# A second expert whose output product becomes seven block products in a phase of its own per token group

## The chip, the cores and the metric

The kernel runs on one core of one Trainium2 chip, as one launch. The metric is the device time of that launch in microseconds (us); the runs shown are medians. TensorE is called PE, VectorE DVE, ScalarE ACT, GpSimd POOL, and SyncE, which issues the DMAs, SP.

## What is computed

Attention without a softmax, then two experts one after the other on 2304 tokens of 512 values. All inputs and outputs are float32:

```python
ret = scores * Dmat                       # batch 4, 8 heads, 576 tokens, 64 values a head
x = transpose(ret @ v)                    # 2304 tokens x 512
h = x @ w_in                              # first expert, 2048 hidden
x = (h * cos(h)) @ w_out
xn = x / sqrt(mean(x * x) + 1e-6) * rms_g # second expert, 1536 hidden
silu = g * sigmoid(g)  where  g = xn @ w_gate
out = (silu * (xn @ w_val)) @ w_out
```

## The kernel before

**Precision.** Each float32 factor is split into a rounded high part (a cast on ACT) and the rest (a subtraction on DVE, the helper `minus`, line 124). A product is three matmuls: high by high, high by low, low by high.

**Stages.** Attention comes first. The first expert then takes the tokens in five tiles (four of 512, one of 256); in its second and third tile it also turns the second expert's weights from 64-bit words into float32 values, which it stores in DRAM (`piece_steps`). In the last tile of the first expert (five steps of ACT and DVE work beside each hidden block, `other_steps`, from a list `ready`) the second expert's first operands and weights are made.

**Second expert, gate and value.** Three groups of 768 tokens, each in two halves of 384. A group has twelve *quads* `q`, even ones for the gate, odd ones for the value. A quad gives two blocks of 128 hidden features by two token halves, from 512 inputs, and does this 2x2 block product with seven block products (line 745) in place of eight: six matmuls of 384 columns each. They go to two PSUM banks, alpha and beta. Between them alpha is copied out by ACT (s1, s2, s4; line 752), DVE adds a sum to a bank (lines 765 and 772), ACT applies Silu (767) and DVE multiplies by it (773). Where a product starts a bank anew, or adds to it after a copy, it waits for the reader. A quad's weights are three plain blocks and four sums, each as high and low part (768 KB and 1024 KB). In group 0 they are made while the quads run, two ahead (`quad_steps`: casts lines 509 and 524, subtractions, four small sums on DVE), and stored; groups 1 and 2 load them again (543), one quad ahead, into two sides.

**Second expert, output.** After each gate and value pair `j`, the four products are split into high and low parts (777, 124), and the pair's output product is 36 matmuls of 512 columns (`out_n`, line 717), into six banks that stay open through the group. They are emitted in pieces between the products of the *next* two quads (`fills`): nine, nine, nine, and the rest.

**Order.** In the second expert PE, ACT, DVE and POOL are given their instructions in the order of the code; only between the two parts of the program may rows move. SP's DMAs are placed by a scheduler. An engine runs its row strictly in order, so a waiting instruction holds those behind it.

## Time and profile before

| | |
|---|---|
| Median of 3 runs | 926.82 us (925.85 to 929.55) |
| Profiled execution, span | 923.1 us (first to last instruction; 3.7 us below the median of the runs) |
| PE busy | 900.4 us, 98% of the span, 4996 matmuls |
| DVE, ACT, POOL busy | 615.7, 462.1, 29.3 us |
| Second expert | 493.49 us to the end |
| Granted clock of TensorE | 0.999 of its full 2.4 GHz |

A row of the timeline gives start, length, engine, line, operation and count; `[0.57 <-ACT s L752]` is idle time before it and what ended it. Matmuls overlap: a matmul's length is longer than the distance to the next start, and the distance is the pace.

### The profile page before, as it was taken

Reading aid. Unit: us, or ns where it says so; the run is one execution under the profiler, and the core shown is the slowest. Engines: PE = TensorE matmul, PEld = TensorE weight load, DVE = VectorE, ACT = ScalarE, POOL = GpSimd, SP = SyncE. Lnnn points to the kernel's source line nnn. Section 1 sums busy time; section 2 is a strip of 40 time slices with the busy share of each in tenths; the row PEclk is TensorE's granted clock in tenths of the full one; section 3 lists DMA queues with packets and bytes.
Section 4 is the critical chain, followed back from the end, with each engine's and each line's share of the span. In section 5 each row is a group of like instructions: output and inputs, shape, how many; then the busy total and the mean of one; then the engine's idle time right before and its main releaser. Section 6 shows DMA issues by size and latency. Waiting matters only on the chain.

```text
span 923.1 us, 12892 instructions
## 1 busy us (share of the span) xinstructions
PE 900.4 (98%) x4996; PEld 789.8 (86%) x4996; DVE 615.7 (67%) x1022; ACT 462.1 (50%) x816; POOL 29.3 (3%) x27
## 2 busy tenths in 40 slices
PE   7899999999999999999999999999999999999998
PEld 6788888888887888988887899999888999999997
DVE  3999989678888887668667666675456445333332
ACT  4666576576556665467544444444342334322222
POOL 2321100000000000000000000000000000000000
PEclk9999999999999999999999999999999999999999
DMA  9966261136525443202045376666744555755531
GB/s 333 411 222 252 98 251 47 34 126 195 170 68 173 146 157 115 62 2 102 1 173 181 141 300 252 252 264 248 253 181 177 207 204 215 264 206 206 206 129 68
DMA packets 34732, 163.72 MB, mean 177 GB/s; under 512 B 4080, under 2 KB 5232, under 8 KB 23792
## 3 DMA queue, kind: packets, MB, share of 16 engines
q1 hardware_dynamic: 34672, 162.91, 48.5%
q8 instruction: 39, 0.64, 0.3%
q14 instruction: 21, 0.17, 0.1%
HBM read 123.57 MB, written 39.32 MB: 176 GB/s over the span
## 4 chain that ended last, share of the span: by engine, by line
PE 66%; DVE 24%; ACT 6%; issue 3%; DMA 1%; SPq 0%; ACTq 0%; DVEq 0%
PE h L745 27%; PE acc L717 16%; PE acc L187 6%; PE acc L188 6%; PE acc L189 6%; DVE t L142 3%; DVE r L422 3%; DVE r L416 2%; DVE glo L124 2%; DVE t L143 2%; ACT ghi L424 2%; PE h L189 2%; PE h L187 2%; PE h L188 2%; DVE t L137 2%
## 5 line engine op out<-in xcount | busy, mean ns | idle before, releaser
L745 PE MATMUL h<-w 128*128 128x384 f32 x1224 | 230.5, 337 | 6.6 <-ACT s L752 2.6
L745 PEld LDWEIGHTS h<-w 128*128 128x128 f32 x1224 | 215.0, 188 | 15.2 <-ACT s L752 5.3
L717 PE MATMUL acc<-w,shi 128*128 128x512 f32 x432 | 134.4, 392 | 0.0
L187 PE MATMUL acc<-ghi,w 128*128 128x512 f32 (+1 forms) x320 | 117.4, 373 | 2.9 <-ACT xall L615 1.9
L188 PE MATMUL acc<-glo,w 128*128 128x512 f32 (+1 forms) x320 | 117.8, 369 | 0.1
L189 PE MATMUL acc<-ghi,w 128*128 128x512 f32 (+1 forms) x320 | 117.4, 368 | 0.0
L752 ACT COPY s<-h 128x384 f32<-128x384 f32 x108 | 51.8, 479 | 128.0 <-PE h L745 127.9
L717 PEld LDWEIGHTS acc<-w,shi 128*128 128x128 f32 x432 | 80.1, 188 | 13.5
L418 ACT ACTIVATE r<-r,half_pi 128x512 f32<-128x512 f32 (+1 forms) x80 | 54.5, 681 | 68.7 <-DVE r L416 68.2
L765 DVE TENSOR_TENSOR sg<-s,h 128x384 f32<-128x384 f32 x54 | 29.9, 553 | 85.4 <-PE h L745 45.7
L717 PE MATMUL acc<-w,slo 128*128 128x512 f32 x216 | 85.4, 395 | 0.0
L777 ACT CAST shi<-v 128x384 fp32r<-128x384 f32 x72 | 37.1, 515 | 70.0 <-DVE v L773 70.0
L187 PEld LDWEIGHTS acc<-ghi,w 128*128 128x128 f32 x320 | 59.4, 188 | 14.7 <-ACT xall L615 2.9
L124 DVE TENSOR_TENSOR glo<-r,ghi 128x512 fp32r<-128x512 f32 (+1 forms) x78 | 49.6, 636 | 33.5 <-ACT ghi L424 31.7
L424 ACT CAST ghi<-r 128x512 fp32r<-128x512 f32 (+1 forms) x80 | 46.2, 578 | 50.7 <-DVE r L422 49.5
L188 PEld LDWEIGHTS acc<-glo,w 128*128 128x128 f32 x320 | 60.3, 188 | 10.2 <-DVE glo L124 0.3
L189 PEld LDWEIGHTS acc<-ghi,w 128*128 128x128 f32 x320 | 60.3, 189 | 10.1
L124 DVE TENSOR_TENSOR slo<-v,shi 128x384 fp32r<-128x384 f32 x72 | 40.1, 557 | 37.3 <-ACT shi L777 37.3
L772 DVE TENSOR_TENSOR v<-s,h 128x384 f32<-128x384 f32 x54 | 29.8, 552 | 52.0 <-PE h L745 37.9
L745 PE MATMUL h<-b,w 128*128 128x384 f32 x288 | 56.7, 338 | 0.0
L188 PE MATMUL h<-xlo,w 128*128 128x512 f32 (+1 forms) x148 | 54.3, 367 | 0.1
L189 PE MATMUL h<-xhi,w 128*128 128x512 f32 (+1 forms) x148 | 54.2, 366 | 0.0
(105 smaller groups left out, 1514.2 us busy)
## 6 DMA issues: line engine op xcount, KB each, us to landing
w<-s SPq DMA_DIRECT2D x24, 1024.0 KB, 4.8
raw<-w_dram SPq DMA_DIRECT2D x36, 512.0 KB, 4.0
w<-w SPq DMA_DIRECT2D x18, 1024.0 KB, 5.0
w<-s SPq DMA_DIRECT2D x24, 768.0 KB, 6.4
raw<-w_dram SPq DMA_DIRECT2D x16, 1024.0 KB, 7.3
x<-qkv_dram SPq DMA_DIRECT2D x15, 1024.0 KB, 11.5
s<-w SPq DMA_DIRECT2D x12, 1024.0 KB, 4.8
s<-w SPq DMA_DIRECT2D x12, 768.0 KB, 3.7
```

The lines of the kernel that those rows point to most:

```text
L124: eng.tensor_tensor(dst, src, hi.bitcast(F32), op=ALU.subtract)
L187: nc.tensor.matmul(dst, a[0], b[0], start=start, stop=False)
L188: nc.tensor.matmul(dst, a[0], b[1], start=False, stop=False)
L189: nc.tensor.matmul(dst, a[1], b[0], start=False, stop=stop)
L418: nc.scalar.activation(r, r, AF.Sin, bias=half_pi, scale=1.0)
L424: nc.scalar.copy(hi, r)
L717: nc.tensor.matmul(acc, (hi, hi, lo)[k][:, c], w[:, u, (0, 1, 0)[k], :], start=start and u == 0 and k == 0, stop=stop and u == 1 and k == 2)
L745: nc.tensor.matmul(bank, a[:, wp], xp[:, c], start=start and kc == 0 and n == 0, stop=kc == 1 and n == 2, skip_group_check=True)
L752: nc.scalar.copy(t, alpha)
L765: nc.vector.tensor_tensor(t, s, bank, op=ALU.add)
L772: nc.vector.tensor_tensor(t, s, bank, op=ALU.add)
L777: nc.scalar.copy(hi, t)
```

## The change

The output product now also is a 2x2x2 block product done with seven block products, once per token group after its twelve quads (`whole_out`). The three halved dimensions are the tokens (two halves of 384), the hidden features (the two blocks of each pair) and the outputs (two halves of 256). One block product (`out_product`) is six feature blocks by three token blocks by three parts: 54 matmuls of 256 columns. The group's 24 gated blocks are kept in a float32 tile `SV`; `out_split` makes the high and low parts of two of its blocks (768 columns), and `out_difference` makes four differences over the tile (128x2304 each), three on DVE and one on POOL. `block_out` adds the sums and sends the output; `s1`, `s2`, `s4` are as in a quad.

The output weights are made once, as three plain blocks and four sums of each pair, in the last tile of the first expert (`out_steps`, six of them, ahead of the steps for quads 0, 1 and 2) and stored in DRAM as seven parts of 1536 KB. The small sums move from DVE to POOL. There are now three sides; `fetch(n + 3)` loads quads and output parts alike, three items ahead. Quads have no fills: `quad` stops twice (`yield`), and the loop runs quad `q`'s products 3 to 5, then products 1 and 2 of quad `q+1`, then products 6 and 7 of `q`; neighbours use two different pairs of banks. The normalisation steps for later groups go in at the hooks.

```diff
         yield
-        if before is not None:
-            minus(nc.vector, w[:, 1].bitcast(F32R), hi, z)
-            nc.sync.dma_start(store[before // 2][:, before % 2], w.bitcast(F32))
         yield
...
+    def operand_weights(q, plain, sums, keep):
+
+        def high0():
+            z = values_of[q]
+            nc.scalar.copy(plain[:, 0], z[:, :3])
+
+        def low0():
+            z = values_of[q]
+            minus(nc.vector, plain[:, 1], plain[:, 0], z[:, :3])
+            for dst, a, b, op in ((4, 0, 3, ALU.subtract), (3, 3, 2, ALU.add), (0, 3, 0, ALU.subtract), (1, 1, 0, ALU.subtract)):
+                nc.gpsimd.tensor_tensor(z[:, dst], z[:, a], z[:, b], op=op)
+
+        def high1():
+            z = values_of[q]
+            for n in range(2):
+                nc.scalar.copy(sums[:, 0, 2 * n:2 * n + 2], z[:, 3 * n:3 * n + 2])
+
+        def low1():
+            z = values_of.pop(q)
+            for n in range(2):
+                minus(nc.vector, sums[:, 1, 2 * n:2 * n + 2], sums[:, 0, 2 * n:2 * n + 2], z[:, 3 * n:3 * n + 2])
+            keep()
+
+        return [("A", high0), ("D", low0), ("A", high1), ("D", low1)]
...
+    def out_steps(j):
+
+        plain = late["pw"].tile([P, 2, 3, 2 * P], F32R, tag="pw", name="pw")
+        sums = slots[0].rearrange("p a b c -> p (a b c)").rearrange("p (h n c) -> p h n c", h=2, n=4)
+
+        def keep():
+            for n, part in enumerate([plain[:, :, n] for n in range(3)] + [sums[:, :, n] for n in range(4)]):
+                nc.sync.dma_start(kept_out[OUT_PLACES[n]][:, :, j], part.bitcast(F32))
+            fetch_next()
+
+        return operand_weights(3 * j + 2, plain, sums, keep)
...
-    def ahead(n):
...
+    def ahead(i, n):
...
+        if 0 < n <= 2 * NPR:
+            j, half = divmod(n - 1, 2)
+            if not half:
+                late["out"] = out_steps(j)
+            ready.extend(late["out"][2 * half:2 * half + 2])
+        if 1 <= n < 8:
             ready.append(late["steps"].pop(0))
             while late["steps"] and late["steps"][0][0] != "A":
                 ready.append(late["steps"].pop(0))
...
+        if n in (11, 13, 14):
+            late["quad"] = quad_steps((11, 13, 14).index(n))
+            ready.extend(late["quad"][:2])
+        if n in (12, 13, 14):
+            ready.extend(late["quad"][2:])
...
+    while ready:
+        ready.pop(0)[1]()
...
+        alpha, beta = (t[:, :HALF] for t in banks())
...
+            dst = SV[:, j, u, h]
...
+                    nc.vector.tensor_tensor(dst, s, bank, op=ALU.add)
+                nc.scalar.activation(dst, bank if s is None else dst, AF.Silu)
+            else:
+                if s is not None:
+                    t = gp.tile([P, HALF], F32, tag="v", name="v")
                     nc.vector.tensor_tensor(t, s, bank, op=ALU.add)
...
+                    bank = t
+                nc.vector.tensor_tensor(dst, bank, dst, op=ALU.mult)
...
         product(alpha, plain[:, :, 0], 0, True)
-        s1 = keep("s1")
-        also("s1")
+        s1 = sums_of("s1", alpha)
         product(beta, plain[:, :, 1], 1, True)
-        r11 = result(0, 0, s1, beta)
-        next(r11)
-        also("m11")
+        result(0, 0, s1, beta)
+        hook("r11")
+        yield
         product(alpha, sums[:, :, 0], 2, False)
-        s2 = keep("s2")
-        next(r11)
-        also("r11")
+        s2 = sums_of("s2", alpha)
+        hook("s2")
         product(beta, sums[:, :, 3], 3, True)
         product(alpha, sums[:, :, 2], 4, False)
-        s4 = keep("s4")
-        also("s4")
-        r22 = result(1, 1, s4, beta)
-        next(r22)
-        also("m22")
-        next(r22)
-        also("r22")
-        fills(9)
+        s4 = sums_of("s4", alpha)
+        result(1, 1, s4, beta)
+        hook("r22")
+        yield
         product(alpha, sums[:, :, 1], 5, False)
-        r12 = result(0, 1, None, alpha)
-        next(r12)
-        next(r12)
+        result(0, 1, None, alpha)
         product(beta, plain[:, :, 2], 6, False)
-        r21 = result(1, 0, s2, beta)
-        next(r21)
-        also("m21")
-        next(r21)
-        fills(9 if q % 2 == 0 else 36)
-        also("end")
-
-    fill = []
...
+    def out_split(k, i):
+        a, b = BLOCK_OF[k]
+        src = SV[:, 2 * i:2 * i + 2, a, b, :]
+        t = places.pop(0)
+        split_out.setdefault(k, []).append(t)
+        nc.scalar.copy(t[:, 0], src)
+        minus(nc.vector, t[:, 1], t[:, 0], src)
+
+    def out_difference(eng, dst, a, b):
+        x = lambda ab: SV[:, :, ab[0], ab[1], :]
+        eng.tensor_tensor(x(dst), x(a), x(b), op=ALU.subtract)
+
+    def out_product(g, k, pair, start):
+
+        n = g * ITEMS + NQUAD + OUT_ORDER.index(k)
+        w = side_out(n)
+        home = split_out.pop(k)
+
+        def product(i, m):
+            s, wi = home[i // 2], w[i // 3][:, :, i % 3]
+            bank = pair[m // 2][:, m % 2 * 2 * P:(m % 2 + 1) * 2 * P]
+            for p, (a, b) in enumerate(((0, 0), (0, 1), (1, 0))):
+                nc.tensor.matmul(bank, s[:, a, i % 2, m * P:(m + 1) * P], wi[:, b],
+                                 start=start and i == 0 and p == 0 and m % 2 == 0, stop=i == NPR - 1 and p == 2,
+                                 skip_group_check=True)
+
+        last = g == NGROUP - 1 and k == OUT_ORDER[-1]
+        for i, m in [(i, m) for m in range(3) for i in range(NPR)] if last else [(i, m) for i in range(NPR) for m in range(3)]:
+            product(i, m)
+        places.extend(home)
+        fetch(n + 3)
...
+    def whole_out(g):
+
+        s = operand_steps(g + 1) if g + 1 < NGROUP else []
+        alpha, beta = [acc_tile(0), acc_tile(1)], [acc_tile(2), acc_tile(3)]
+        out_product(g, 0, alpha, True)
+        out_split(1, 2)
+        for i in range(3):
+            out_split(5, i)
+        s1 = sums_out("s1", alpha)
+        out_difference(nc.vector, (0, 0), (0, 1), (0, 0))
+        out_difference(nc.vector, (0, 1), (1, 1), (0, 1))
+        out_difference(nc.vector, (1, 1), (1, 1), (0, 0))
+        out_difference(nc.gpsimd, (1, 0), (1, 0), (1, 1))
+        out_product(g, 1, beta, True)
+        for i in range(3):
+            out_split(2, i)
+        block_out(g, 0, 0, s1, beta)
+        gamma = banks()
+        out_product(g, 5, gamma, True)
+        for i in range(3):
+            out_split(3, i)
+        out_product(g, 2, alpha, False)
+        for i in range(3):
+            out_split(4, i)
+        s2 = sums_out("s2", alpha)
+        out_product(g, 3, beta, True)
+        for i in range(3):
+            out_split(6, i)
+        plus(s2, s2, beta)
+        run(s[:9])
+        out_product(g, 4, alpha, False)
+        s4 = sums_out("s4", alpha)
+        block_out(g, 0, 1, s4, gamma)
+        block_out(g, 1, 1, s4, beta)
+        run(s[9:16])
+        delta = banks()
+        out_product(g, 6, delta, True)
+        block_out(g, 1, 0, s2, delta)
+        run(s[16:])
+
+    for g in range(NGROUP):
+
+        pending = []
+
+        def hook(q, at):
...
+            if g == 0 and 0 < q < NQUAD - 2 and at in ("s2", "r21"):
+                if at == "s2":
+                    pending[:] = quad_steps(q + 2)
+                run(pending[:2])
+                del pending[:2]
+            if q in (5, 10) and at == "r22":
+                out_split(0, q // 7)
+            if q == NQUAD - 1:
+                if at == "r11":
+                    out_split(0, 2)
+                elif at == "r22":
+                    out_split(1, 0)
+                    out_split(1, 1)
+            elif g < 2:
+                idle(1, "P") if at == "s2" else None
+                idle(2, "AD")
...
+        now = quad_of(0)
+        next(now)
+        for q in range(NQUAD):
+            next(now)
+            then = quad_of(q + 1) if q + 1 < NQUAD else None
+            if then:
+                next(then)
+            next(now)
+            now = then
...
+        if g + 1 < NGROUP:
+            assert len(normal) == (3, 5)[g], (g, normal, len(background))
+        whole_out(g)
```

**PE, the second expert's first quads and an output phase.** Before: quads 0 and 1 and most of 2 in one run on banks `h`, then the output product in pieces.

```order
L189 MATMUL acc<-ghi,w 128x512
L745 MATMUL h<-w 128x384 x114
L717 MATMUL acc<-w,shi 128x512 x2
L717 MATMUL acc<-w,slo 128x512
L717 MATMUL acc<-w,shi 128x512 x2
L717 MATMUL acc<-w,slo 128x512
L717 MATMUL acc<-w,shi 128x512 x2
L717 MATMUL acc<-w,slo 128x512
L745 MATMUL h<-w 128x384 x12
L717 MATMUL acc<-w,shi 128x512 x2
L717 MATMUL acc<-w,slo 128x512
L717 MATMUL acc<-w,shi 128x512 x2
```

Now: quads alternate between the bank pairs `h` and `acc`; the last 30 are products 3 to 7 of quad 11, and behind them stand the 378 matmuls of the output phase of 256 columns.

```order
L194 MATMUL acc<-ghi,w 128x512
L763 MATMUL h<-w 128x384 x30
L763 MATMUL acc<-w 128x384 x12
L763 MATMUL h<-w 128x384 x12
L763 MATMUL acc<-w 128x384 x18
L763 MATMUL h<-w 128x384 x12
L763 MATMUL acc<-w 128x384 x12
```

```order
L763 MATMUL h<-w 128x384 x18
L763 MATMUL acc<-w 128x384 x12
L763 MATMUL h<-w 128x384 x12
L763 MATMUL acc<-w 128x384 x30
L828 MATMUL acc<-w 128x256 x18
L828 MATMUL acc<-w,b 128x256 x18
L828 MATMUL acc<-w 128x256 x72
L828 MATMUL h<-w 128x256 x54
L828 MATMUL acc<-w 128x256 x18
```

The pieces between the quads are gone, and the matmuls of 256 columns stand behind the whole group.

**ACT, the start of the second expert.** Before (`z` holds weight values; `w` are quad 2's weights, made last; quads 0 and 1 were made earlier):

```order
L424 CAST ghi_4417<-r_4416 128x512
L653 ACT_TABLE_LOAD
L653 ACTIVATE spare_83<-half_pi_81 128x1
L509 CAST w_4446<-z_4339 128x768
L524 CAST w_4460<-z_4339 128x512 x2
L752 COPY s1_4524<-h_4516 128x384
L752 COPY s2_4540<-h_4516 128x384
L767 ACTIVATE sg_4532<-sg_4532 128x384
L752 COPY s4_4555<-h_4516 128x384
L615 COPY xall_84<-acc_3935 128x512
L767 ACTIVATE sg_4558<-sg_4558 128x384
```

Now (`w_4308`, `w_4359` quad 0; `w_3937<-z_4435` the last output block; `w_4404`, `w_4459` quad 1; `w_4550` quad 2):

```order
L682 ACT_TABLE_LOAD
L682 ACTIVATE spare_83<-half_pi_81 128x1
L514 CAST w_4308<-z_4491 128x768
L525 CAST w_3937<-z_4435 128x512 x2
L525 CAST w_4359<-z_4491 128x512 x2
L748 COPY s1_4637<-h_4629 128x384
L773 ACTIVATE SV_4628<-SV_4628 128x384
L748 COPY s2_4653<-h_4629 128x384
L748 COPY s4_4667<-h_4629 128x384
L773 ACTIVATE SV_4628<-SV_4628 128x384
L644 COPY xall_84<-acc_3921 128x512
L514 CAST w_4404<-z_4534 128x768
```

The casts of quad 0 now stand directly ahead of its first copy, and those of quad 1 behind quad 0's fourth bank copy, a Silu and a copy to `xall`.

**ACT, a gate quad followed by a value quad.** Before, in group 1 (`s1` to `s4` of both quads, Silu on `sg`, casts of the products `shi`):

```order
L752 COPY s1_5922<-h_5914 128x384
L752 COPY s2_5938<-h_5914 128x384
L767 ACTIVATE sg_5930<-sg_5930 128x384
L752 COPY s4_5953<-h_5914 128x384
L767 ACTIVATE sg_5955<-sg_5955 128x384
L767 ACTIVATE sg_5973<-h_5914 128x384
L767 ACTIVATE sg_5981<-sg_5981 128x384
L752 COPY s1_6014<-h_6006 128x384
L752 COPY s2_6031<-h_6006 128x384
L777 CAST shi_6033<-v_6022 128x384
L752 COPY s4_6049<-h_6006 128x384
L777 CAST shi_6059<-v_6051 128x384
```

Now, at the end of group 0, quads 10 (`h_5320`) and 11 (`acc_5393`); the casts from `SV` to `b_5366` and `w_3990` are `out_split(0, 1)` and `(0, 2)`:

```order
L525 CAST w_3937<-z_5217 128x512 x2
L748 COPY s2_5373<-h_5320 128x384
L748 COPY s4_5387<-h_5320 128x384
L773 ACTIVATE SV_4628<-SV_4628 128x384
L811 CAST b_5366<-SV_4628 128x768
L748 COPY s1_5401<-acc_5393 128x384
L811 CAST w_3990<-SV_4628 128x768
L773 ACTIVATE SV_4628<-h_5320 128x384
L773 ACTIVATE SV_4628<-SV_4628 128x384
L748 COPY s2_5437<-acc_5393 128x384
L748 COPY s4_5451<-acc_5393 128x384
```

The copies s1 and s2 of the value quad now stand behind a cast of 768 columns each, and s2 behind the gate quad's last two Silus as well.

## Rows read from the trace of the kernel before

**Rows 1.** Page, part 1: busy us, share of the span, instructions.
```profile
PE 900.4 (98%) x4996; PEld 789.8 (86%) x4996; DVE 615.7 (67%) x1022; ACT 462.1 (50%) x816; POOL 29.3 (3%) x27
```

**Rows 2.** Lines by form, PE: shapes, count, busy us, mean ns, idle before.
```profile
L745 PE MATMUL h<-w 128*128 128x384 f32 x1224 | 230.5, 337 | 6.6 <-ACT s L752 2.6 <-DVE sg L765 2.5 <-DVE v L772 0.9
L717 PE MATMUL acc<-w,shi 128*128 128x512 f32 x432 | 134.4, 392 | 0.0
...
L717 PE MATMUL acc<-w,slo 128*128 128x512 f32 x216 | 85.4, 395 | 0.0
L745 PE MATMUL h<-b,w 128*128 128x384 f32 x288 | 56.7, 338 | 0.0
```

**Rows 3.** Timeline, PE, second expert in full swing: start us, length.
```profile
523.73 0.63 PE L717 MATMUL acc<-w,shi 128*128 128x512 f32 x2
...
525.81 5.41 PE L745 MATMUL h<-w 128*128 128x384 f32 x30
531.06 0.63 PE L717 MATMUL acc<-w,shi 128*128 128x512 f32 x2
```

**Rows 4.** Timeline, PE, first expert's tile of 256 tokens.
```profile
363.89 0.28 PE L187 MATMUL h<-xhi,w 128*128 128x256 f32 x1
...
366.77 0.28 PE L187 MATMUL acc<-xhi,w 128*128 128x256 f32 x1
```

**Rows 5.** Timeline, PE, start and end of the second expert.
```profile
493.49 5.70 PE L745 MATMUL h<-w 128*128 128x384 f32 x30
499.76 3.40 PE L745 MATMUL h<-w 128*128 128x384 f32 x18 [0.57 <-ACT s L752]
...
519.54 0.63 PE L717 MATMUL acc<-w,shi 128*128 128x512 f32 x2
...
919.20 0.39 PE L717 MATMUL acc<-w,slo 128*128 128x512 f32 x1
```

**Rows 6.** Lines by form, ACT.
```profile
L752 ACT COPY s<-h 128x384 f32<-128x384 f32 x108 | 51.8, 479 | 128.0 <-PE h L745 127.9
...
L767 ACT ACTIVATE sg<-sg 128x384 f32<-128x384 f32 x54 | 28.4, 526 | 28.8 <-DVE sg L765 28.5
...
L562 ACT CAST w<-xall 128x768 fp32r<-128x768 f32 x17 | 14.1, 829 | 0.0
L524 ACT CAST w<-z 128x512 fp32r<-128x512 f32 x24 | 13.7, 618 | 14.1 <-DVE z L518 14.1
```

**Rows 7.** Lines by form, DVE.
```profile
L773 DVE TENSOR_TENSOR v<-v,sg 128x384 f32<-128x384 f32 x54 | 30.1, 558 | 1.9
...
L124 DVE TENSOR_TENSOR w<-xall,w 128x768 fp32r<-128x768 f32 x17 | 16.3, 956 | 1.7 <-ACT w L562 1.5
```

**Rows 8.** Timeline, PE and ACT, near the end.
```profile
899.72 2.27 PE L745 MATMUL h<-w 128*128 128x384 f32 x12
901.04 0.48 ACT L752 COPY s<-h 128x384 f32<-128x384 f32 x1 [2.09 <-PE h L745]
```

**Rows 9.** Timeline, POOL and DVE, attention stage.
```profile
36.27 1.08 POOL L244 TENSOR_TENSOR x<-x,gk_sb 128x512 f32<-128x512 f32 x1 [4.24 <-DMA x<-qkv_dram]
...
36.49 1.95 DVE L142 SCALAR_TENSOR_TENSOR t<-raw,t 128x1024 int32<-128x1024 int32 x1
...
46.86 1.23 DVE L142 SCALAR_TENSOR_TENSOR t<-raw,t 128x1024 int32<-128x1024 int32 x1
```

**Rows 10.** DMA issues: count, KB each, median us from issue to landing.
```profile
w<-s SPq DMA_DIRECT2D x24, 1024.0 KB, 4.8
...
w<-s SPq DMA_DIRECT2D x24, 768.0 KB, 6.4
...
z<-w SPq DMA_DIRECT2D x12, 512.0 KB, 5.7
```

**Rows 11.** Windows: engines' busy us, granted clock, DMA share, GB/s.
```profile
480.00:493.00 13.00, 13.00 (x59) 10.78 (x58) 10.28 (x18) 8.04 (x12) 0.00 (x0) 1.00 0.66 250
520.00:535.00 15.00, 15.00 (x79) 13.90 (x78) 11.89 (x23) 6.24 (x13) 0.00 (x0) 1.00 0.86 333
```

More of the change, by code (lines that the diff above doesn't have):

```diff
@@ L536, in quad_steps @@
[L536 to L548 removed]
+        def keep():
+            for part, dst in zip((plain, sums), kept[q]):
+                nc.sync.dma_start(dst, part.bitcast(F32))
+            fetch_next()
```

324 lines of the change are left out of this document (131 added, 193 removed).

## The prediction

> **What bounds the kernel now.** I read the page's shares first: PE is busy 900.4 of 923.1 us, against 615.7 for DVE, 462.1 for ACT and 29.3 for POOL [rows 1]. So the time is PE's work plus the holes in it. The timeline of PE gives the paces that the work is made of [rows 3]: nine matmuls of 512 columns between 523.73 and 525.81, 0.231 us each, and thirty of 384 between 525.81 and 531.06, 0.175 us each. Changes of shape inside a stretch cost nothing that shows.
>
> The second expert starts at 493.49; its last matmul ends at 919.20 + 0.39 = 919.59 [rows 5], so it lasts 426.1 us. It holds 1224 + 288 = 1512 matmuls of 384 columns and 432 + 216 = 648 of 512 [rows 2]: 1512 x 0.175 + 648 x 0.231 = 264.6 + 149.7 = 414.3 us. Waits are the remaining 11.8 us. The lines by form name what ended them: ACT's copies, DVE's sums [rows 2]. 114 matmuls stand before 519.54: 26.05 us for 19.95 of work [rows 5], so 6.1 of the 11.8 lie in the first three quads, and 5.7 in all the rest.
>
> **PE's work after.** The 1512 stay. The 648 go, and 3 groups x 7 products x 54 = 1134 of 256 columns come. The only rows with that width are in the first expert: 24 in 366.77 - 363.89 = 2.88, or 0.120 us each [rows 4]. Then 1134 x 0.120 = 136.1, against 149.7: **13.6 us less**. The break-even is 149.7 / 1134 = 0.132 us. Bounds for the pace: half of 512's, 0.1155 (another 5 us gained), and 384's, 0.175 (62 lost); I take 0.120, from the same width.
>
> A rule speaks against this step. The Trainium skill, "TensorE: Matmul & The Clock Gate", section "Back-to-back issue gap", gives 81 ns sustained for 128 columns and 131 ns for 512; a straight line between them gives an estimate of 98 ns for 256. By it the new work is 1134 x 0.098 = 111 us and the old 648 x 0.131 = 85, so the change would add 26 us in place of taking 13.6. The trace does not agree with these figures: 512 columns take 231 ns here and 256 take 120.
>
> **What the fills covered.** A product of six is 6 x 0.175 = 1.05 us. A bank's result is visible 0.27 us after its product's nominal end: the six of the row at 899.72 end at 900.77, the copy starts at 901.04 [rows 8]. Copies take 0.48, Silu 0.53, a cast of 768 columns 0.83, of 512 columns 0.62, a subtraction of 768 columns 0.96, an add of 384 about 0.56 [rows 6, 7]. A copy therefore frees its bank 0.27 + 0.48 after the product. The next product in that bank stands one product later (1.05) in the run 3, 4, 5: nothing lost if ACT is free. Now 36 matmuls of 512 columns no longer stand between; two products of the neighbour quad do, 2.1 us.
>
> *A. The first quads.* PE reaches quad 0 with no weights lying ready; before, two quads had them. Taken along ACT's new row: quad 0's first cast waits for its values, whose load takes 5.7 us [rows 10] and is issued behind the output blocks' stores: 1.5 lost (0 to 4). The second cast, behind POOL's small sums: 1.0. Quad 1's cast stands behind quad 0's s4 copy, a Silu and the copy to `xall`: 0.27 + 0.48 + 0.56 + 0.53 + about 0.6, then 0.83 for the cast and 0.96 for the low part [rows 6, 7], 4.2 in all, of which 3.9 on PE. Quad 3's cast waits for its load in front of quad 1's copies: 1.8. With 0.3 of small ones 8.5 (bounds 5 to 12) in place of 6.1: **+2.4**.
>
> *B. Group 0's value quads 3, 5, 7 and 9.* ACT has a Silu and two weight casts ahead of s2: 0.27 + 0.56 + 0.53, then 2 x 0.62, then the copy, 3.0 to 3.1 after the third product, where the fifth wants it after 2.1 (the neighbour's two lie between). 0.9 x 4 = **+3.6** (0, if the Silu's input is early, to 6).
>
> *C. Each group's end.* Quad 11 has no neighbour behind it. ACT's row between its first products is the cast of `out_split(0, 2)` (0.83), then its low part on DVE (0.96), the add (0.56), the Silu (0.53), s2 (0.48): the copy is done about 4.0 after the third product where 2.1 is there, 1.9 lost; the sixth product then waits 0.27 + 0.48 for s4, 0.75. In `whole_out` ACT's casts have 6.48 us a product (54 x 0.120), far more than they need. DVE has three differences of 2304 columns: 0.558 for 384 [rows 7], and from 384 to 768 columns 0.398 more (956 - 558), so 0.558 + 5 x 0.398 = 2.54 each. The POOL difference is 4.5 times the 512-wide row of 1.08 [rows 9], 4.9. I get the low part of block 2 ready 27.9 us after quad 11's third product starts, where PE wants it at 27.6: 0.3. That is 1.9 + 0.75 + 0.3 = 2.9, three times: **+8.7** (0, if quad 11's queue is hidden, to 15).
>
> *D. The rest.* The old 5.7 us go with the order they came from; the normalisation steps at the hooks are still there, so I keep 2.0: **-3.7** (-5.7 to 0).
>
> **Costed at nothing.** The output weights' casts, subtractions and seven stores per pair in the first expert's last tile: PE fills 13.00 of 13.00 us there, with DVE at 10.28 and ACT at 8.04 [rows 11], so each has 2.7 to 5 us in 13 free. If that cover is short, 0 to 3 lost. The last output is read from its bank and stored as before.
>
> **Weights.** Groups 1 and 2 load every quad as before, 768 + 1024 KB (1.835 MB), but a quad now lasts 7 x 1.05 = 7.35 us: 250 GB/s. The two are issued together and the later lands after 6.4 us [rows 10], 287 GB/s. An output part is 1.573 MB in 6.48 us, 243 GB/s. In 520 to 535 us, 333 GB/s went through at a share of 0.86 [rows 11], and a side is requested three items ahead, about 10.5 us before its use. So nothing is lost.
>
> **Sum.** -13.6 + 2.4 + 3.6 + 8.7 - 3.7 = -2.6. The profiled execution's span is 923.1, so 920.5 after. The median of the runs, 926.8, lies 3.7 above that span: 924.2 us.
>
> **The rivals.**
>
> *R1, fewer waits.* B and the shortfall in `whole_out` do not come: ACT's idle time before its copies is nearly all waiting for PE, 127.9 of 128.0 us over 108 copies [rows 6], so ACT runs early. Against it: those idles lie where the fills were. Then only the start at its old 6.1 and quad 11's 2.6 x 3 = 7.8 remain, 13.9 in place of 11.8: 926.8 - 13.6 + 2.1 = 915.3.
>
> *R2, late weights, slower.* In groups 1 and 2 the weight stream sets the pace, from where it gives under 250 GB/s. For it: one load of 1024 KB takes 4.8 us, 218 GB/s [rows 10], and 480 to 493 moved 250 [rows 11], the very rate needed. Against it: 287 and 333. At 230, between 218 and the 243 that output parts need, a quad lasts 7.98 us: 0.63 x 24 = 15, so 939.
>
> *R3, POOL holds DVE.* In the attention stage POOL's instruction of 1.08 us began at 36.27, a DVE operation with two SBUF inputs at 36.49; it took 1.95 where its like takes 1.23 [rows 9]. It seems to stand until POOL's ends, 37.35. If that holds for all small sums and for a difference that takes twice my 4.9, it costs 3 us at each group's end and about 0.5 in each of twelve quads of group 0 ahead of the low weight parts: 9 + 6 = 15, less the 5 that A to C hold of it already: 924.2 + 10 = 934. Against it: over 10 DVE steps in `whole_out` have 45.4 us, of which some 40 are used.
>
> The Trainium skill, "SBUF — State Buffer", section "SBUF: two separate sides", says that the port which VectorE and GpSimd share is an exclusive lock; whoever starts first has it for its whole instruction. The pair at 36.27 and 36.49 agrees; 1.23 becomes 1.95.
>
> *R4, no gain in 256 columns.* At 0.175 a matmul the change costs 198.5 - 149.7 = 49 us: 973. The row of 0.120 speaks against it; only that it lies in another stage keeps it open.
>
> **Chances.** The forecast 0.46, with a range of its own of 918 to 929 (A to D moved by half their bounds); R1 0.27; R2 0.13; R3 0.12; R4 0.02. 912 to 938 leaves out a quarter of R1, half of R2, a quarter of R3 and R4: 0.185. Half a per cent, 4.6 us, is about what a measurement of this kernel tells from no change. Faster (under 922.2): 0.16 of the forecast and 0.26 of R1, 0.42. Same: 0.30, 0.01, 0.01 of R2 and 0.03 of R3, 0.35. Slower (over 931.4): 0.12, 0.09 and 0.02, 0.23.
>
> **What would show it.** In the timeline of PE, 54 matmuls of 256 columns in 6.48 us, if 0.120 holds; over 7.1, and the gain is gone. The second expert's matmuls by line should sum to about 401 us of pace, with 8.5 us of holes in the first four quads, ended by weight parts. Quad 11 should show a hole of about 2 us before its fifth product, ended by ACT's s2, in each group; if not, R1. Holes before the first product of quads in groups 1 and 2, ended by a DMA, mean R2. A DVE subtraction far over 0.96 beside a POOL row in `whole_out` means R3. The forecast is wrong if the holes after the first quads sum to less than 8 us or to more than 20.

## The result, and the profile after

The changed kernel takes 934.2 us (median of 4 runs, 933.08 to 936.55) where the kernel before takes 926.71: a ratio of 1.0078, 95% interval 1.0058 to 1.0098. The forecast was 924.2, a little faster, in a range of 912 to 938; the kernel got 7.5 us slower, which lies in the range but the other way from the forecast.

First the page, busy time by engine, as [rows 1]:

```profile
PE 894.3 (96%) x5482; PEld 808.3 (87%) x5482; DVE 682.7 (73%) x1010; ACT 476.0 (51%) x813; POOL 116.3 (12%) x102
```

PE is busy 6 us less in a span that is 8.6 longer (931.7 for 923.1). So the work shrank and the waits grew. (The profiled execution of the kernel before was the fastest of its runs, 925.85, so the spans differ by more than the medians.) The pace of the new matmuls, in a stretch of PE's timeline without waits (start, length, count):

```profile
627.44 17.43 PE L828 MATMUL acc<-w 128*128 128x256 f32 x144
644.71 2.26 PE L828 MATMUL acc<-w,b 128*128 128x256 f32 x18
```

144 matmuls take 17.27 us, 0.120 each, the value taken from [rows 4]. PE's waits by line, with shapes, as [rows 2]:

```profile
L763 PE MATMUL acc<-w 128*128 128x384 f32 x720 | 141.7, 344 | 14.1 <-ACT s L748 10.4 <-ACT w L514 2.9 <-DVE v L777 0.8
L763 PE MATMUL h<-w 128*128 128x384 f32 x720 | 137.2, 339 | 4.9 <-ACT s L748 3.9 <-DVE SV L772 0.8 <-DVE w L129 0.2
L828 PE MATMUL acc<-w 128*128 128x256 f32 x846 | 103.7, 283 | 1.5 <-DVE w L129 1.5
```

No transfer ends a wait of PE there: all are ACT's copies and casts and a few DVE steps. Where they lie is seen in PE's timeline at the start of the second expert, as [rows 5]:

```profile
492.15 0.50 PE L192 MATMUL acc<-ghi,w 128*128 128x512 f32 x1 [0.56 <-ACT ghi L431]
493.22 0.50 PE L193 MATMUL acc<-glo,w 128*128 128x512 f32 x1 [0.57 <-DVE glo L129]
...
495.83 0.51 PE L763 MATMUL h<-w 128*128 128x384 f32 x2
496.54 2.03 PE L763 MATMUL h<-w 128*128 128x384 f32 x10 [0.19 <-DVE w L129]
500.95 3.78 PE L763 MATMUL h<-w 128*128 128x384 f32 x18 [2.38 <-ACT s L748]
507.64 4.56 PE L763 MATMUL acc<-w 128*128 128x384 f32 x12 [2.92 <-ACT w L514]
512.00 2.98 PE L763 MATMUL h<-w 128*128 128x384 f32 x12
514.83 3.28 PE L763 MATMUL acc<-w 128*128 128x384 f32 x18
```

Two things are to be seen. The stage starts at 495.83 in place of 493.49, behind two holes in the first expert's last output product, and then has holes of 2.38 and 2.92. Not all of the 2.34 is the holes': the first matmul of the last hidden block, 60 matmuls before the stage, is late already (the kernel before, then the changed one):

```profile
479.89 0.39 PE L187 MATMUL h<-xhi,w 128*128 128x512 f32 x1
480.54 0.39 PE L192 MATMUL h<-xhi,w 128*128 128x512 f32 x1
```

So 0.65 was there before, and the holes cost 1.7. Such a difference comes from far ahead and says nothing of the edits: the 1500th matmul before the stage starts at 188.86 here, and in the profiles of the experiments, none of which edits anything ahead of it, from 187.98 to 196.07. A start is therefore compared from the rows above: 13.6 us later in the kernel before, 15.3 in the changed one.

And the twelve matmuls at 507.64 take 4.36 us, 0.363 each: half speed. The windows tell why (columns as [rows 11]; the third figure from the end is the granted clock):

```profile
507.00:512.00 5.00, 4.36 (x12) 3.87 (x13) 3.11 (x4) 1.59 (x3) 3.12 (x4) 0.50 0.57 230
512.00:516.00 4.00, 4.00 (x20) 4.00 (x20) 3.48 (x6) 2.12 (x5) 0.94 (x1) 0.81 0.47 184
523.00:527.00 4.00, 3.71 (x13) 3.71 (x14) 3.71 (x8) 1.55 (x3) 1.58 (x2) 0.60 0.97 295
742.00:746.00 4.00, 3.85 (x13) 3.85 (x14) 3.32 (x5) 1.56 (x3) 0.00 (x0) 0.57 0.16 11
```

In the first window the clock stands at its lower level, 1.2 GHz, after PE had idled 2.92 us and, before that, 2.38; it is still low in part of the second, and low again in part of 523 to 527, behind holes of 0.99 and 0.77, and of 742 to 746, behind holes of 1.55 and 0.62 at the end of group 1. Of a matmul row the loss against the pace (next start less its own, less count times 0.1736 or 0.120) holds both: idle time and a low clock. Summed over the second expert it gives this, beside the terms of the prediction:

| term | before | predicted | measured |
|---|---|---|---|
| PE's work, at 0.175, 0.231 and 0.120 a matmul | 414.3 | 400.7 | 400.7 |
| A, losses to 530 us | 6.1 | 8.5 | 13.5, of it 4.7 at low clock |
| B, quads 3, 5, 7, 9 | | 3.6 | 2.8 |
| C, three groups' ends | | 8.7 | 11.4, of it 1.7 at low clock |
| D, the rest | 5.7 | 2.0 | 4.4 |
| later start of the stage | | 0 | 2.3, of it 1.7 in the two holes |

Losses of 32.1 in place of 11.8, less 13.6 of work, and the 2.3: the span's 8.6 within 0.4. The paces limit how exact this is: at 0.1736 the work is 398.6, and 2 us of small losses then stand in no row.

A group's end, PE and ACT (quad 11's products 3 to 7, then the output phase):

```profile
594.83 2.24 PE L763 MATMUL acc<-w 128*128 128x384 f32 x12
598.63 1.32 PE L763 MATMUL acc<-w 128*128 128x384 f32 x6 [1.55 <-ACT s L748]
600.58 2.38 PE L763 MATMUL acc<-w 128*128 128x384 f32 x12 [0.62 <-ACT s L748]
```

```profile
595.36 0.84 ACT L811 CAST w<-SV 128x768 fp32r<-128x768 f32 x1 [1.70 <-DVE SV L779]
596.11 0.48 ACT L773 ACTIVATE SV<-h 128x384 f32<-128x384 f32 x1
597.69 0.52 ACT L773 ACTIVATE SV<-SV 128x384 f32<-128x384 f32 x1 [1.10 <-DVE SV L772]
598.12 0.46 ACT L748 COPY s<-acc 128x384 f32<-128x384 f32 x1
```

The cast of 768 columns waits 1.70 for DVE; two Silus stand behind it, and s2 last, as the changed order has them. PE's hole behind it is 1.55, 1.55 and 1.54 in the three groups.

Last, the chain of work that ended last, between 480 and 535 us (start, length, what):

```profile
482.90 5.69 DMA z<-w
488.60 0.07 issue
488.67 0.32 POOL z L520
488.99 5.64 DMA z<-w
494.66 0.84 ACT w L514
```

Loads of weight values make half of this chain in that stretch (also 5.77 from 513.94, 5.17 from 521.80, 5.68 from 528.02). Behind the casts and sums of the last output blocks the values of quads 0 and 1 come late.

### The profile page after: what moved, and what is told of

It is laid out like the page before. It is cut to its first block, busy times and chain, and to the rows that moved or that the text cites. A ratio compares the mean times of both kernels' runs of the same rounds, so it can differ in the third digit from the quotient of the medians.

```text
span 931.7 us, 14276 instructions
## 1 busy us (share of the span) xinstructions
PE 894.3 (96%) x5482; PEld 808.3 (87%) x5482; DVE 682.7 (73%) x1010; ACT 476.0 (51%) x813; POOL 116.3 (12%) x102
## 4 chain that ended last, share of the span: by engine, by line
PE 64%; DVE 21%; ACT 5%; DMA 5%; issue 3%; SPq 1%; POOL 1%; ACTq 0%; DVEq 0%; POOLq 0%
PE acc L828 10%; PE h L763 10%; PE acc L763 10%; PE acc L192 7%; PE acc L193 7%; PE acc L194 7%; DVE w L129 4%; DMA z<-w 3%; PE h L193 3%; PE h L192 3%; PE h L194 3%; DVE t L147 2%; DVE r L429 1%; DMA x<-qkv_dram 1%; DVE glo L129 1%
## 5 line engine op out<-in xcount | busy, mean ns | idle before, releaser
L763 PE MATMUL acc<-w 128*128 128x384 f32 x720 | 141.7, 344 | 14.1 <-ACT s L748 10.4
L763 PEld LDWEIGHTS acc<-w 128*128 128x128 f32 x720 | 128.5, 193 | 19.4 <-ACT s L748 14.5
L763 PE MATMUL h<-w 128*128 128x384 f32 x720 | 137.2, 339 | 4.9 <-ACT s L748 3.9
L763 PEld LDWEIGHTS h<-w 128*128 128x128 f32 x720 | 127.2, 191 | 7.7 <-ACT s L748 5.2
L828 PE MATMUL acc<-w 128*128 128x256 f32 x846 | 103.7, 283 | 1.5 <-DVE w L129 1.5
L828 PEld LDWEIGHTS acc<-w 128*128 128x128 f32 x846 | 102.4, 192 | 2.0 <-DVE w L129 2.0
L520 POOL TENSOR_TENSOR z<-z 128x256 f32<-128x256 f32 x72 | 69.8, 972 | 163.5 <-DMA z<-w 112.9
L777 DVE TENSOR_TENSOR v<-s,acc 128x384 f32<-128x384 f32 x54 | 29.8, 552 | 52.8 <-ACT s L748 43.7
L129 DVE TENSOR_TENSOR w<-SV,w 128x768 fp32r<-128x768 f32 x55 | 58.9, 1118 | 9.9 <-ACT w L811 9.0
L772 DVE TENSOR_TENSOR SV<-s,h 128x384 f32<-128x384 f32 x54 | 29.8, 552 | 41.6 <-ACT s L748 29.2
L811 ACT CAST w<-SV 128x768 fp32r<-128x768 f32 x55 | 42.6, 833 | 29.1 <-DVE SV L779 14.8
```

Of the source, the lines that this page charges most:

```text
L129: eng.tensor_tensor(dst, src, hi.bitcast(F32), op=ALU.subtract)
L520: nc.gpsimd.tensor_tensor(z[:, dst], z[:, a], z[:, b], op=op)
L763: nc.tensor.matmul(bank, a[:, wp], xp[:, c], start=start and kc == 0 and m == 0, stop=kc == 1 and m == 2, skip_group_check=True)
L772: nc.vector.tensor_tensor(dst, s, bank, op=ALU.add)
L777: nc.vector.tensor_tensor(t, s, bank, op=ALU.add)
L811: nc.scalar.copy(t[:, 0], src)
```

## The experiments

All times are medians, all ratios against the kernel before run on the same chip with them. The first theory: the losses have separate causes, an order of ACT's row at a group's end, POOL beside DVE, and weights that are late for the first quads since output blocks stand ahead of them; the rivals are in each expectation.

**1. Quad 11's cast behind s2.**

```diff
-                if at == "r11":
+                if at == "s2":
                     out_split(0, 2)
```

> Edit: in quad 11 the cast of 768 columns that makes the output operand stands behind the copy s2 on ACT instead of in front of it. Theory (that cast, which waits for quad 11's first result, holds s2): the hole of 1.55 us before the fifth product (1.72 lost against the pace) falls below 0.4 in all three groups, and with it the slow matmuls after it in group 1 (1.67 lost); the hole of 0.62 before the sixth stays: 3 x 1.4 to 3 x 1.4 + 1.7, so 928 to 930. Rival (the two Silus of quad 10, still in front of s2, and the DVE sum that they wait for hold it): the hole keeps 0.8 or more, gain under 2.5, 931.7 or more.

Measured: 929.39 us, 1.0025 (1.0009 to 1.0041). PE's timeline at the same place:

```profile
594.13 3.31 PE L763 MATMUL acc<-w 128*128 128x384 f32 x18
598.05 2.37 PE L763 MATMUL acc<-w 128*128 128x384 f32 x12 [0.62 <-ACT s L748]
```

Products 3, 4 and 5 are one run of 18; only the hole of 0.62 is left. The theory holds, and the two Silus, which still stand in front of s2, cost nothing here. This kernel starts the second expert with the same holes (2.40 and 2.92), and its profiled execution shows that the clock need not fall:

```profile
507.00:512.00 5.00, 2.94 (x15) 2.62 (x16) 2.77 (x3) 1.63 (x3) 2.47 (x4) 1.00 0.69 265
```

Of four profiles with this start (the changed kernel, this one, experiment 2, and the two edits together in experiment 5) three have the low clock there; and in the changed kernel the holes of 1.55 and 0.62 had it behind them in group 1 alone, not in groups 0 and 2. So the low clock is a risk of such holes, not a sure price; over the 12 runs of this kernel the time goes from 934.61 at a mean clock of 0.989 to 927.08 at 0.996.

**2. The fourth difference on DVE.** In the changed kernel POOL's difference and one DVE subtraction stand side by side:

```profile
617.26 5.20 POOL L816 TENSOR_TENSOR SV<-SV 128x2304 f32<-128x2304 f32 x1 [30.79 <-DVE SV L816]
```

```profile
617.99 5.28 DVE L129 TENSOR_TENSOR w<-SV,w 128x768 fp32r<-128x768 f32 x1 [0.91 <-PE h L828]
623.19 0.95 DVE L129 TENSOR_TENSOR b<-SV,b 128x768 fp32r<-128x768 f32 x1
```

```diff
-        out_difference(nc.gpsimd, (1, 0), (1, 0), (1, 1))
+        out_difference(nc.vector, (1, 0), (1, 0), (1, 1))
```

> Edit: the fourth difference of the output phase (2304 columns) on DVE instead of POOL. In the changed kernel one DVE subtraction of 768 columns took 5.28 us beside POOL's row of 5.20, where its like takes 0.96, and PE then waited 0.77 us for a low part in two of three groups. Theory (POOL's instruction holds DVE's until it ends, 4.3 us, which is more than the 2.5 us that the difference takes on DVE): no DVE row over 1.3 us there, the holes of 0.77 go, gain 0.9 to 2.8, 931.4 to 933.3. Rival (DVE is simply full in that stretch, whoever takes the difference): the holes stay or grow, 934 or more.

Measured: 933.53, 1.0058 (1.0036 to 1.0079). Four differences on DVE, then:

```profile
615.61 10.33 DVE L816 TENSOR_TENSOR SV<-SV 128x2304 f32<-128x2304 f32 x4
625.87 0.95 DVE L129 TENSOR_TENSOR w<-SV,w 128x768 fp32r<-128x768 f32 x1
```

No DVE subtraction of 768 columns in the output phases takes over 1.1 us, and PE has no hole there: the mechanism is as expected. The time is 0.2 us outside the theory's range, and the gain against the changed kernel, some 2 us by the ratios, is within their intervals.

**3. Half of the output blocks' conversions.**

```diff
-        if 0 < n <= 2 * NPR:
+        if 0 < n <= NPR:
...
-                nc.sync.dma_start(kept_out[OUT_PLACES[n]][:, :, j], part.bitcast(F32))
+                for to in (j, j + NPR // 2):
+                    nc.sync.dma_start(kept_out[OUT_PLACES[n]][:, :, to], part.bitcast(F32))
...
-        if n in (11, 13, 14):
+        if n in (9, 11, 13):
```

> Edit: only three of the six output weight blocks are converted in the first expert's last tile (the other three get copies of them, so half of the second output product has wrong weights); the stores stay as many, and quads 0, 1 and 2 are started two to four steps earlier. Theory (the first quads are late because the six blocks stand ahead of them in the list of ACT and DVE work): the holes at the end of the first expert (2.3 us later start) and in the first quads (13.5 us lost against the pace) fall to the 6 us that the kernel before had, or less: gain 7 to 10, 924 to 927. Rival (the transfers are the limit there: 363 GB/s at 500 to 507 us; the stores are unchanged): gain under 3, over 931.

Measured: 922.05, 0.9949 (0.9931 to 0.9968). PE's start:

```profile
494.13 2.27 PE L764 MATMUL h<-w 128*128 128x384 f32 x12
498.20 3.39 PE L764 MATMUL h<-w 128*128 128x384 f32 x18 [1.79 <-ACT s L749]
501.43 2.24 PE L764 MATMUL acc<-w 128*128 128x384 f32 x12
```

One hole of over a microsecond is left, and the stage starts on time, 13.6 us behind the matmul named above. To 530 us the losses are 2.9 in place of 13.5; with the 1.7 of the later start that is 12 us in this one place, more than the theory's 7 to 10. The three blocks' loads, casts and sums are left out together here, so this shows their price as a whole, and not which of them sets it. These conversions, which the prediction put at nothing, are the main loss.

**4. All conversions, half of their stores.**

```diff
-            for n, part in enumerate([plain[:, :, n] for n in range(3)] + [sums[:, :, n] for n in range(4)]):
+            for n, part in enumerate([plain[:, :, n] for n in range(3)] + [sums[:, :, n] for n in range(4)] if j < NPR // 2 else []):
```

> Edit: all six output weight blocks are converted as in the changed kernel, but only the first three are stored (5.25 MB less to write; the second half of each output product reads the first half's weights, so its result is wrong). The counterpart of the half outputs, which kept the stores and left out the conversions, and gained 12 us. Theory A (the transfers limit the start: their share is 1.03 in 500 to 507 us, and values and stores share them): the late values come early, gain 7 or more, 927 or less. Theory B (the chain of loads, casts, sums on POOL and subtractions, two steps of the tile for each block, limits it): gain under 4, over 930.

Measured: 929.07, 1.0022 (1.0005 to 1.0040), 5 us less than the changed kernel: neither theory's figure. The two holes at the first expert's end are gone (the stage starts 13.6 us behind the matmul named above). The stores are a part of it, and the conversions with the loads the larger part.

**5. Another order: quads 0 and 1 ahead of output blocks 4 and 5.**

```diff
+        if n == 11:
+            ready.extend(quad_steps(1))
-        if 0 < n <= 2 * NPR:
-            j, half = divmod(n - 1, 2)
+        if 0 < n <= 8 or 11 <= n < 15:
+            j, half = divmod(n - 1 if n < 9 else n - 3, 2)
```

> Edit: the same work in another order: output blocks 0 to 3, then the weights of quads 0 and 1, then output blocks 4 and 5, then quad 2. Theory (as for the half outputs: what matters is that quads 0 and 1 are ready when PE reaches them, and output blocks 4 and 5 have 100 us until they are used): 3 to 8 us, 926 to 931. Rival (ACT, DVE and POOL or the transfers have no room for two blocks more beside the first quads, and quad 2 or 3 comes as late as quad 1 did): the holes move, gain under 2, 932 or more.

Measured: 933.42, 1.0084 (1.0052 to 1.0117). The rival: quad 0 starts with both its weights, has holes of 1.41 and 0.74, and one of 8.22 us follows in quad 1, ended by a DVE sum that stands in DVE's row behind the low parts of the output blocks. With the two edits of 1 and 2:

> Edit: the new order of the last tile, the cast of quad 11 behind s2, and the fourth difference on DVE, together. Theory: the three causes are separate and their gains add: 3 to 8, 4.8 (measured alone) and 0.9 to 2.8, so 919 to 925, faster than the kernel before. Rival (what is gained at the start is given back in the group by holes that the late start covered, or by a clock that is low for as long): 928 or more.

Measured: 924.78, 0.9969 (0.9955 to 0.9982); the timeline has the same hole:

```profile
509.57 1.20 PE L765 MATMUL acc<-w 128*128 128x384 f32 x6
518.99 4.26 PE L765 MATMUL acc<-w 128*128 128x384 f32 x12 [8.22 <-DVE v L779]
```

Without the new order:

> Edit: the cast of quad 11 behind s2 and the fourth difference on DVE, without the new order of the last tile. If the gains add, 934.2 - 4.8 - 0.7 to 2.8: 926.6 to 928.7. The three together gave 924.8, and the order alone 0.8 us: if it is near 925, the order does nothing; if 927 or more, the order is worth 2 or more here.

Measured: 925.15, 0.9987 (0.9968 to 1.0006). So the order does nothing that can be measured, and the two edits make the changed kernel as fast as the one before.

**6. The half outputs with the two edits.**

> Edit: the half outputs together with the cast of quad 11 behind s2 and the fourth difference on DVE (half of the output product has wrong weights). This shows what is left of the change's gain in PE's work once the start is on time and the two holes at a group's end are gone. Theory (the gains add): 922.05 - 4.8 - 0.7 to 2.8, 914.4 to 916.6, which is 11 to 12 us under the kernel before, near the 13.6 us of work that the 256-column products save. Rival (new holes take the place of those removed): 919 or more.

Measured: 914.35, 0.9853 (0.9829 to 0.9877): the gains add. With the start on time and the ends mended, the ratio is worth 13.6 us, what the count of the block products promises, though only with half of the output blocks made.

**7. The links of the chain at the start, one by one.** The staging tile (a), POOL's sums (b), loads behind stores (c):

```diff
-        plain = late["pw"].tile([P, 2, 3, 2 * P], F32R, tag="pw", name="pw")
+        plain = late["pw"].tile([P, 2, 3, 2 * P], F32R, tag="pw", name="pw") if j < NPR - 1 else side(1)[0]
```

> Edit: the last output block's plain parts go to a weight buffer that is free by then, so that ACT's cast no longer waits 4.19 us for the stores out of the one staging tile. Theory (ACT's row order and POOL's sums set the start, not the staging tile): the two holes at the end of the first expert (0.56 and 0.57 us) go, the second expert starts near 494 in place of 495.8, but quad 0's cast still waits for its values, which landed at 494.6: the whole gains 0 to 1.5 us, 932.7 to 934.2. Rival (the staging tile is the head of the whole late start, since quad 1's values are asked for only behind its stores): 4 to 6 us, 928 to 930.

Measured (a): 935.16, 1.0085 (1.0061 to 1.0109): no gain, which is on the theory's side. The holes at the first expert's end are gone; ACT then waits 3.18 us for the values, where it had waited 1.05.

```diff
-                nc.gpsimd.tensor_tensor(z[:, dst], z[:, a], z[:, b], op=op)
+                nc.vector.tensor_tensor(z[:, dst], z[:, a], z[:, b], op=op)
```

> Edit: the four small sums of each weight block on DVE, as in the kernel before, instead of POOL. Theory (POOL's 1.1 us a sum delays the second casts: ACT waited 2.85, 3.41 and 2.28 us for them): the hole of 2.38 us in quad 0 falls to about 1, quad 1's 2.92 partly, with less of the half clock behind them: gain 4 to 7, 927 to 930. Rival 1 (POOL's instructions hold DVE's throughout): gain 10 or more, under 924.5. Rival 2 (only ACT's row order counts): under 2, over 932.

Measured (b): 934.61, 1.0081 (1.0059 to 1.0103): the figure of rival 2, though DVE's row counts as well. The hole of 2.38 becomes 1.27 and that of 2.92 becomes 1.30, but holes of 0.92 and 1.59 come at the first expert's end, where the sums now stand in DVE's row, and 1.91 and 1.48 behind.

```diff
+            fetch_next()
             for part, dst in zip((plain, sums), kept[q]):
                 nc.sync.dma_start(dst, part.bitcast(F32))
-            fetch_next()
```

> Edit: when a weight block is done, the load of the values of the block after the next is asked for ahead of its stores, not behind them (SP's row then has it in front of the last three stores of an output block, and of a quad's stores). In the changed kernel the chain of work that ended last goes through loads of values: 5.69 us from 482.90, 5.64 from 488.99, 5.77 from 513.94, 5.17 from 521.80, 5.68 from 528.02. Theory (with two value tiles the start is a chain of load, casts, subtractions, and the next load, and each link has stores ahead of its load): each link gets 1 to 3 us shorter, PE's losses to 530 us fall by 4 to 8, 926 to 930. Rival (the transfers share one capacity, so what the load gains the stores lose, or ACT's row order decides): gain under 2, over 932.

Measured (c): 934.22, 1.0078 (1.0066 to 1.0090): the rival's figure. The loads do land earlier (a median of 4.2 us after issue between 480 and 535, where it was 5.7, while stores of 1024 KB go from 4.8 to 7.8); PE then waits 3.27 and 3.70 behind POOL's sums. With the edits of 1 and 2 the same step gave 925.18, 0.9978 (0.9963 to 0.9992), where 917 to 921 was expected: also nothing against 925.15 without it. All three links:

> Edit: the load ahead of the stores, the small sums on DVE and the last output block's plain parts in a free buffer, all at once, with the two edits at the group's end (which gave 925.15 without these three). Each of the three alone gave nothing: 934.2, 934.6 and 935.2 us. Theory (the start is a chain in which several links are nearly as long: with one shortened the next takes over; after the load came first, the chain that ended last went through POOL's sums for 19% of 480 to 535 us and the stores out of the staging tile for 8%): all three together shorten it, 919 to 923. Rival (the sum of the work of ACT, DVE and transfers sets it, so order and place don't matter): 924 or more.

Measured: 923.44, 0.9957 (0.9940 to 0.9974). That is 1.7 us by the medians under the version without them, 2.8 by the ratios, with intervals that overlap: it lies between the two theories and does not decide.

**8. Two output blocks in the middle of group 0**.

```diff
-        if 0 < n <= 2 * NPR:
+        if 0 < n <= 8:
...
+    LATE = {1: (4,), 3: (0,), 4: (1, 5), 6: (0,), 7: (1,)}
...
+            if g == 0 and at == "r22":
+                if q in LATE:
+                    for what in LATE[q]:
+                        late_out(what) if what > 3 else run(late["out"][2 * what:2 * what + 2])
```

> Edit: only output weight blocks 0 to 3 are made in the first expert's last tile, at the early places; the weights of quads 0, 1 and 2 follow two to four steps earlier than before; blocks 4 and 5 are made between the products of quads 1 to 7 of group 0, with the still empty part of the tile of gated blocks as their staging; with the cast of quad 11 behind s2 and the fourth difference on DVE. The whole result is computed. Theory (the two kinds of work don't have to meet at the start; the middle of group 0 has room, with ACT busy 36 of 67 us and DVE 47 of 67 at 530 to 597): 914.4, as with half the outputs, and 1 to 5 us for four steps in ACT's row and 4.6 MB more transfers in group 0: 915 to 920. Rival (the chain of conversions and stores is full through all of group 0, with a transfer share of 0.85, so the work only moves): 923 or more, as with the three edits (924.8).

Measured: 927.90, 1.0005 (0.9994 to 1.0016). Quad 0 is on time, then:

```profile
508.00 4.11 PE L773 MATMUL h<-w 128*128 128x384 f32 x12 [6.88 <-DVE SV L782]
...
550.79 1.32 PE L773 MATMUL acc<-w 128*128 128x384 f32 x6 [1.69 <-ACT s L758]
...
570.62 1.33 PE L773 MATMUL acc<-w 128*128 128x384 f32 x6 [1.70 <-ACT s L758]
```

Losses of 9 us to 530, and against the same pace 11 between 530 and 597 us, where the half outputs lose 3 in the same quads (530 to 583): the rival, the work comes back. With quad 2's second steps behind quad 0's last result:

> Edit: as the late outputs, but the second half of quad 2's weight steps (the cast of sums, which stood in ACT's row behind quad 0's first copy and waited there 5.15 us for POOL, while DVE and PE waited for ACT) is put behind quad 0's last result. In the late outputs this place cost a hole of 6.88 us and 1.9 more at half clock. Theory (the start is then on time, and the rest of the price of making everything lies in group 0, where holes ended by ACT's copies came to 9.7 us in place of 3.0): 927.9 - 7 to 9, 919 to 921, faster than the kernel before. Rival (the chain stays full and the same time is lost at quads 1 to 3): 924 or more.

Measured: 925.57, 0.9985 (0.9966 to 1.0004), the rival's figure; the hole is 4.60 in place of 6.88. And with the load ahead of the stores:

> Edit: the load ahead of the stores in the version that makes output blocks 4 and 5 in the middle of group 0. Theory (its two prices, 6.5 us at the start and 9.7 in group 0, are late loads as well): 925.57 less 4 to 8, 917 to 922. Rival (ACT's and DVE's order there, with steps of normalisation in front, sets both): under 2, over 923.5.

Measured: 922.45, 0.9954 (0.9941 to 0.9967). The hole at the start is 3.51, and the clock stayed up. It is the fastest complete version, 0.46% under the kernel before. The time lies between the two ranges; by the ratios the earlier load gained 3 us here, with intervals that just meet.

**9. PE kept busy in the holes.** Twelve and sixteen more matmuls of 384 columns that nobody reads:

```diff
+        if (g, q) == (0, 0):
+            warm_up(12)
         product(alpha, sums[:, :, 0], 2, False)
```

> Edit: 12 matmuls of 384 columns more in quad 0's hole before its third product and 16 more before quad 1's first, into a bank that the next product overwrites, so PE is busy where it stood idle; the holes' causes stay. Theory (the half clock of 507 to 512 us and the 0.81 of 512 to 516 follow from the idle time before them): the granted clock stays at 1.00 there and the 2.28 + 0.75 us lost against the pace come back, perhaps also part of what is lost at 522 to 530: 929.5 to 931.5. Rival (the clock falls for another reason, or the extra work costs as much as it gives): 934 or more.

Measured: 936.76, 1.0112 (1.0084 to 1.0139). The clock stayed at 1.00 from 500 to 516 us; but a cast of quad 2 moved in ACT's row, ahead of a Silu, and waited 4.19 us for POOL's sums, which made a hole of 4.48 on PE at 521.04. As a test of the clock's price it is spoiled; the profile of experiment 1 beside that of the changed kernel tells more.

**10. No interleave.** Each quad's seven products in one run.

```diff
-            then = quad_of(q + 1) if q + 1 < NQUAD else None
-            if then:
-                next(then)
-            next(now)
-            now = then
+            for _ in quad_of(q):
+                pass
```

> Edit: each quad's seven products in one run, the next quad behind it, on alternating bank pairs as in the changed kernel; so a product that waits for a bank has no neighbour's products in front of it. Quad 11, which has none behind it now, loses 1.72 + 0.91 us. Theory (the neighbour covers about as much in every quad): 36 quads at 0.9 to 2.6 us, 30 to 90 more, and more at half clock: 965 to 1030. Rival (ACT is early except at quad 11): under 950.

Measured: 966.46, 1.0404 (1.0375 to 1.0433).

```profile
865.33 5.38 PE L763 MATMUL h<-w 128*128 128x384 f32 x30
871.33 1.31 PE L763 MATMUL h<-w 128*128 128x384 f32 x6 [0.62 <-ACT s L748]
872.48 1.21 PE L763 MATMUL h<-b,w 128*128 128x384 f32 x6
873.53 5.38 PE L763 MATMUL acc<-w 128*128 128x384 f32 x30
```

In group 2, where no weights are made, every quad lasts 873.53 - 865.33 = 8.20 us in place of 42 x 0.1736 = 7.29: one hole of 0.62, 0.91 lost. So the neighbour's products cover some 32 us by the medians, the theory's lower end.

## Why the prediction was wrong

**The step that failed** is "costed at nothing": the output weights' conversions in the first expert's last tile, with PE at 13.00 of 13.00 us as the evidence and 0 to 3 as the bound. PE was indeed busy there, as in [rows 11], and in the tile itself the two holes cost 1.7, inside the bound. But most of the price does not fall where the work stands; it falls on what is queued behind it. The weights of quads 0 to 2 go through the same two value tiles, casts, sums and stores, and the six blocks push them back. The prediction held a part of this in A (quad 0's values behind the stores, 1.5), so the two belong together: 8.5 and nothing were forecast, 13.5 and 1.7 measured, and with half of the blocks left out 2.9 and nothing (experiment 3). A busy PE beside the added steps shows only that they do not delay the stretch itself; what had to be asked is when the last of them ends, and what waits for its engine, its buffers and its transfers.

**The term that is missing** is the clock: every hole was priced as its idle time alone. In the profiled execution 4.7 us in A and 1.7 in C are matmuls at half clock, 6.4 of the 11.2 by which the span exceeds the forecast's 920.5. The rest is the two holes (1.7) and the 0.65 ahead of them, D (2.4), C without the clock (1.0) and A without it (0.3), less 0.8 that B had too much; that sums to 11.6.

**A** followed ACT's row and was right on the places: the hole in quad 0 behind the second cast, that of quad 1 behind s4, Silu and copy, that of quad 3's casts ahead of s4. It has 8.8 us of holes against 8.5. [Rows 11] show the clock as a column, and it stood at 1.00 there; in the kernel before, the holes of the first quads were under 0.7 us each, so that no row of it showed what a longer hole does.

**B and C** were right in place and near in size: 0.69 for 0.9 four times, 1.72 for 1.9 and 0.90 for 0.75 three times, 0.93 for 0.3 in two of three output phases. Experiment 1 shows the first to be the order of ACT's row; C's excess is the low clock in group 1 (1.67) and the output phases.

**D** was too small by 2.4: 1.23 and 0.93 where the normalisation steps stand, and three holes of 0.5 to 0.6 as a group starts, where DVE still has the last `block_out` and low parts in its row.

**The work** was right: 0.120 us a matmul, so 13.6 us less. The Trainium skill, "TensorE: Matmul & The Clock Gate", section "Back-to-back issue gap", had led to an estimate of 26 us more; the pace of 0.120 refutes it for these operands.

**The rivals.** R1's 915.3 is near the 914.35 of experiment 6, but by luck: there half of the output blocks are missing, the losses to 530 us are 2.9 in place of R1's 6.1, and the first of B's holes (0.52 in quad 3) is there, which R1 leaves out. R2 did not come: in groups 1 and 2 no wait of PE is ended by a transfer. The loads that were late are those of values in group 0. R3's mechanism is real, and stronger than its row: 5.28 us for 0.96, once in each group; as a price it is small, 0.93 twice. That its 934 is the measured time is luck: most of what was lost lies elsewhere. The Trainium skill, "SBUF — State Buffer", section "SBUF: two separate sides", says that the port which VectorE and GpSimd share is held for a whole instruction; the DVE row that ends at 623.27 beside POOL's that ends at 622.46 agrees.

**The sign of being wrong** did not show: the losses after the first quads are 18.6 (16.9 without the low clock), between the 8 and 20 that the prediction set. It watched what comes after the first quads, and more than half of the miss lies in them and ahead of them.

**What stays open** is which link sets the start. Each one shortened alone gave nothing, all three perhaps 2 us, half of the stores left out 5, half of the conversions and their loads 12. That they take over from one another fits, but a limit by the sum of the work fits as well. Open is also what decides whether the clock falls behind a hole, and so what of the 6.4 us another execution pays.

## What to carry to other kernels

Work that is moved into a stretch where the bottleneck is covered is not free: follow the queue behind it (the same engines, staging tiles and loads) to the first thing that the bottleneck will wait for. Holes of a few microseconds on TensorE are dearer than they are long, since the clock may be low behind them. And an operand of the next phase is best cast behind the copies that release banks, not in front of them: one line changed gave 4.8 us here.

## What was not expected of the hardware

The granted clock fell to 0.50 (1.2 GHz) after holes of 2.38 and 2.92 us in one execution and stayed at 1.00 after the same holes in another. A DVE subtraction of two SBUF operands, 0.96 us by itself, took 5.28 beside a POOL subtraction of 2304 columns that had begun 0.73 us before it; it ended 0.81 us after POOL's did.
